# Wider idle products in round 0, later r-u-k sums and conversions, and transposes mixed with conversions in round 1: a linear-attention and MLP kernel on one core

## The chip, the core and the metric

The kernel runs on one core of a Trainium2 chip. The core has a matrix engine (TensorE, "PE" in the profile; its weight loads are listed apart as "PEld"), a vector engine (VectorE, "DVE"), a scalar engine (ScalarE, "ACT"), GpSimd ("POOL") and SyncE ("SP"), which here only issues DMAs. Each engine works through its own queue in order; they wait for each other by semaphores. The metric is the device time of one execution in microseconds, told as the median of several executions.

## What is computed

For every batch (4) and head (8), a recurrence over 768 steps with a state of 48 x 48, then a LayerNorm and a two-layer MLP with a residual:

```python
for t in range(S):
    kt, vt, rt, wt = (k[:, :, t], v[:, :, t], r[:, :, t], w[:, :, t])
    cur = np.einsum('bhd,bhe->bhde', u[None] * kt, vt)
    y[:, :, t] = np.einsum('bhd,bhde->bhe', rt, state + cur)
    state = wt[:, :, :, None] * state + np.einsum('bhd,bhe->bhde', kt, vt)
# x: y with its heads side by side, 4 x 768 x 384
xn = (x - mu) / np.sqrt(var + 1e-06) * g_ln
out = x + np.maximum(xn @ w_ch1, 0.0) @ w_ch2      # 384 -> 1536 -> 384
```

The term with `u` is the "own" term of a step: the sum over d of r, u and k, times v. All of it is in 32-bit floats.

## The kernel before

The time axis is cut into eight **rounds** (four batches, two halves of 384 steps each), and a round into two **units** of four heads. Units are numbered through: round 0 has units 0 and 1 (`u0`, `u1`), round 1 has 2 and 3, round 2 has 4 and 5.

A unit passes these stages. `turned` (line 276) transposes w, k or r of two heads on TensorE (three 128 x 128 products with the identity, names `w_ps`, `k_ps`, `r_ps`) into one of two PSUM banks and copies the result to SBUF on ScalarE (`wT`, `kT`, `rT`). `totals` (line 293) multiplies decays up into six levels (`tot`, `decay`). Then come six **levels**: `quads` (line 366) makes 24 small products of k and r into `a_ps`, `grow` (line 386) multiplies k and r by the decays of the level on VectorE, in place, and `keep` (line 401) copies the valid part of `a_ps` into the matrix `A` with a mask; at the last level these copies are put off to `finish` (ScalarE). `ends` transposes k again (`kn_ps`, `kn`), `states` makes `kv` and runs the recurrence over chunks (`s`), `exchanged` copies states to the other half of the partitions (`sx`), and `outputs` makes `y` and adds the own term (`vo`) into `x`. The own term needs the r-u-k sums: `products` (line 326) multiplies r and k on VectorE (`rk`), `product_sums` (line 340) sums them with u in 12 records of products on TensorE (`own_ps`), which ScalarE copies to `own`. For round 1 on, `moments` and `norm` prepare LayerNorm (`xn`), `turned_x` transposes it (`xT`), and `mlp` (line 562) is a generator that yields after each product group of the MLP: 12 steps for the first layer (`h_ps`, `h`), 12 for the second (`o_ps`, `o`).

The two weight matrices come into the chip in 24 parts. `fetch` (line 218) issues a part's DMA on SP into one of four `raw` buffers. `begin` (line 227) takes three ScalarE operations over a part and then fetches another; `join` (line 244) completes it with three VectorE operations. `converted` sees to it that the parts that an MLP step reads are joined first.

`warm(n)` (line 267) issues n products of zeros, 128 columns each, into a bank that nobody reads.

The order of all work is written out by hand: `InOrder` (line 39) keeps each engine's instructions in program order. Round 0 is written out in lines 648 to 721, with the transposes of round 1 (`ahead`) placed three calls at a time in levels 2 to 5. From round 1 on, a loop (line 731) goes through the levels; the rest of the work of a level is put in a list `tasks`, and `fill` (line 619) spreads it evenly between as many MLP steps as the table `UNTIL` asks for. In round 1 that list holds the `join` and `begin` calls of the level (tables `JOINS` and `BEGINS`, line 730) and then the transposes of round 2 (lines 783 to 790).

SBUF tiles come from pools by tag: `xn` has three buffers, `rk` one, `o` two. A new tile of a tag waits until the last reader of the buffer is done. `products` takes its tiles from `xn`, but the last one of unit 3 from `rk`.

Of the kernel before, what the change touches and what calls it, by code (L numbers as in the profile page):

```python
# [9 lines left out]
F32 = mybir.dt.float32  # L10
# [42 lines left out]
def kernel(  # L53
# [18 lines left out]
    B, H, S, D = r.shape  # L72
    P = 128
# [87 lines left out]
    make_identity(nc, ident)  # L161
    nought = const.tile([P, 1], F32, name="nought")
    DVE.memset(nought, 0.0)
    zeros = nought.broadcast_to([P, P])
    eps = const.tile([P, 1], F32, name="eps")
    DVE.memset(eps, 1e-6)

# [98 lines left out]

    def warm(n):

        ps = ps_m.tile([P, RN], F32, tag="m", name="idle")
        for _ in range(n):  # L270
            PE.matmul(ps[:, 0:P], zeros, zeros, start=True, stop=True)


    st, carry = {}, {}
# [51 lines left out]
    def products(q):  # L326
        a = st[q]
        a["rk"] = []
        for pr in pairs:
            if pr == NP - 1 and q == 2 * U - 1:  # L330
                rk = p1.tile([P, TT, NH, D], F32, tag="rk", name=f"rk{q}_{pr}")
                rk = rk.rearrange("p c h d -> p (c h d)")[:, 0:RN]
            else:
                rk = p3.tile([P, RN], F32, tag="xn", name=f"rk{q}_{pr}")
            DVE.tensor_tensor(
                out=rk, in0=a["r"][:, ts(pr, RN)], in1=a["k"][:, ts(pr, RN)], op=ALU.mult
            )
            a["rk"].append(rk)
# [280 lines left out]
    def fill(until, tasks):  # L619

        n = int(until) - done
        m = max(n, len(tasks))
        for i in range(m):
            for t in tasks[i * len(tasks) // m : (i + 1) * len(tasks) // m]:
                t()
            for _ in range((i + 1) * n // m - i * n // m):
                mlp_step()

    def each(f, *ranges):
        calls = [()]  # L630
        for r_ in ranges:
            calls = [c + (x,) for c in calls for x in r_]
        return [lambda c=c: f(*c) for c in calls]
# [5 lines left out]
    def units_of(rnd):  # L639
        return [U * rnd + g for g in range(U)] if rnd < NR else []  # L640
# [16 lines left out]
    grow(u0, 0)  # L657
    run(each(turned, [u1], "w", pairs))
    totals(0, DVE)
    product_sums(u0)  # L660
    for nm in "rk":
        run(each(turned, [u1], nm, pairs))
        warm(1)
    products(u1)
    quads(u1, 0)
    fetch(2)
# [1 line left out]
    run(each(load_v, [u0, u1], [SPO]) + each(load_vx, [u0, u1], [SPO]))  # L668
    begin()
    begin()  # L670
    grow(u1, 0)
    keep(0, 0)
    ahead = each(turned, new[:1], "wrk", pairs) + each(turned, new[1:], "wrk", pairs)
    for lev in range(1, NLEV):
        for q in (u0, u1):
            quads(q, lev)
        if lev == 1:
            product_sums(u1)
        else:
            run(ahead[3 * lev - 6 : 3 * lev - 3])  # L680
        if lev in (1, 3):
            begin()
        if lev == 5:
            warm(2)
        for which in ("rk",) if lev < NLEV - 1 else "kr":
            for q in (u0, u1):
                grow(q, lev, which)
        keep(0, lev)
# [7 lines left out]
    finish(2)  # L696
    states(u1)
    exchanged(u1)
    product_sums(new[0])
    load(units_of(2)[0], "w", SPO)  # L700
    own_term(u0, DVE)
    begin()
    warm(1)
    outputs(u0)
    product_sums(new[1])
    begin()
    own_term(u1, DVE)
    join()
    warm(1)
    outputs(u1)  # L710
    moments(0)
    load(units_of(2)[1], "w", SPO)
    for q in new:
# [13 lines left out]
        UNTIL.append(UNTIL[-1] + 3)  # L727
    while len(UNTIL) < NR * NLEV:
        UNTIL.append(UNTIL[-1] + MLP_STEPS // NLEV)
    JOINS, BEGINS = (3, 3, 3, 4, 4, 4), (4, 3, 1, 3, 4, 2)  # L730
    for rnd in range(1, NR + 1):
        old, now, new = units_of(rnd - 1), units_of(rnd), units_of(rnd + 1)
        if rnd == 1:
# [1 line left out]
        for lev in range(NLEV):  # L735
# [20 lines left out]
            if rnd == 1:  # L756
                if lev < 2:
                    tasks += each(load, new, "kr"[lev], [SPO])
                if lev == 2:
                    SPO.dma_start(  # L760
                        out=u_bc,
                        in_=bass.AP(
                            tensor=u.tensor, offset=u.offset, ap=[[0, P], [D, H], [1, D]]
                        ),
                    )
                    tasks += each(load_v, now, [SPO])
                if lev == 3:
                    tasks += each(load_vx, now, [SPO])
                if lev in (4, 5):
                    own_term(now[lev - 4], DVE)  # L770
                for i in range(max(JOINS[lev], BEGINS[lev])):
                    tasks += [join] * (i < JOINS[lev]) + [begin] * (i < BEGINS[lev])
            if rnd == 2 and lev == 0:
                tasks += each(load_v, now) + each(load, new, "w")
            if rnd == 2 and lev == 2:
# [5 lines left out]
            if rnd > 2 and lev < 2:  # L781
                tasks += each(load, new, ["w", "kr"][lev])
            first = 3 if rnd == 2 else 1
            if new and first <= lev < first + 3:
                due = each(turned, new, "wkr"[lev - first], pairs)
                if rnd == 1 and lev == 2:
                    due += each(turned, new[:1], "r", pairs)
                if rnd == 1 and lev == 3:
                    due = due[NP:]
                tasks += due  # L790
            if rnd == 2:
                if lev == 0:
                    tasks += each(exchanged, old)
# [17 lines left out]
            if lev == 5:  # L811
# [10 lines left out]
                if rnd >= 2:  # L822
                    tasks += each(own_sums, new[1:]) + each(own_term, new[1:], [POOL])
                    if new:
                        tasks += each(totals, [rnd + 1], [POOL])
            fill(UNTIL[slot], tasks)
            if lev == (2 if rnd == 2 else 4) and old:
                mlps.append(mlp(rnd - 1))
# [32 lines left out]
```

## Time and profile before

| | |
|---|---|
| median of 6 runs | 604.19 us (600.46 to 606.09) |
| the profiled execution | 598.02 us |
| its span, first to last instruction | 596.3 us |
| mean granted TensorE clock | 0.973 of full |
| busy: TensorE, its weight loads | 574.3 us (96%), 392.2 us (66%) |
| busy: VectorE, ScalarE, GpSimd | 295.0 us (49%), 199.6 us (33%), 70.0 us (12%) |
| first `kv` of units 0 and 1 | 46.25 and 48.47 us |
| first `h_ps` (MLP of round 0) | 62.68 us |
| first `y` of round 1 | 123.71 us |

All times inside the execution count from the start of the span. A line of the order of time reads: start, duration, engine, line of the code (here always 49, the helper that keeps the order), operation, tile written and tiles read, shape, number of records, and in brackets the idle time of the engine just before and who ended it. A product of 32-bit floats stands as two records, a transpose as one. Times of products include the latency from their issue to their end, so neighbouring groups overlap a little; distances between starts are the better measure.

### The profile page before, as it was taken

To read this page: it belongs to the slowest core of one execution; us is meant where nothing else is said; L and a number is where in the kernel's file an instruction comes from. 1 tells how busy PE (TensorE), PEld (TensorE's weight loads), DVE (VectorE), ACT (ScalarE), POOL (GpSimd) and SP (SyncE) were. 2 spreads that over 40 slices of the span, in tenths; PEclk is the share of its full clock that TensorE was granted. 3 is DMA by queue.
4 is the path that set the end of the run, shared out by engine and by line. 5 is a ranking of instruction groups with operands and counts; after the bars stand their busy time and mean duration, and the time that the engine had idled before them with its cause. 6 is when DMAs were issued, how large, how long until landed. Compare 5 with 4: busy or idle time off the path is not lost.

```text
span 596.3 us, 19140 instructions
## 1 busy us (share of the span) xinstructions
PE 574.3 (96%) x8550; PEld 392.2 (66%) x8550; DVE 295.0 (49%) x706; ACT 199.6 (33%) x430; POOL 70.0 (12%) x100
## 2 busy tenths in 40 slices
PE   8997989899999999999999999999999999999997
PEld 7887656666667766666666666667666666666554
DVE  3867988989546455445265334626245532130000
ACT  3547767702352215412343114321251015301200
POOL 5000000003170007000240007000230000000000
PEclk8759899999999999999999999999999999999999
DMA  9872788134433412232113402012000000000000
GB/s 160 185 188 69 176 215 204 41 78 88 85 58 60 91 34 41 41 72 58 33 25 62 95 14 55 2 32 58 15 2 4 15 23 6 2 14 26 0 14 26
DMA packets 122129, 36.82 MB, mean 62 GB/s; under 512 B 115776, under 2 KB 118976, under 8 KB 122048
## 3 DMA queue, kind: packets, MB, share of 16 engines
q1 hardware_dynamic: 119648, 35.31, 26.5%
q8 instruction: 67, 1.10, 0.8%
q10 hardware_dynamic: 2400, 0.30, 0.5%
q14 instruction: 14, 0.11, 0.1%
HBM read 28.51 MB, written 4.72 MB: 56 GB/s over the span
## 4 chain that ended last, share of the span: by engine, by line
PE 84%; DVE 8%; ACT 4%; issue 2%; POOL 1%; DVEq 0%; ACTq 0%; POOLq 0%
PE h_ps L49 29%; PE o_ps L49 29%; PE a_ps L49 11%; PE y L49 4%; PE r_ps L49 2%; PE k_ps L49 2%; DVE w_sb L49 2%; PE w_ps L49 2%; PE kv L49 2%; PE kn_ps L49 2%; DVE A L49 1%; PE xT_ps L49 1%; ACT rest L49 1%; DVE rT L49 1%; DVE kT L49 1%
## 5 line engine op out<-in xcount | busy, mean ns | idle before, releaser
L49 PE MATMUL o_ps<-w_sb,h 128*128 128x384 f32 x576 | 197.7, 489 | 0.1
L49 PE MATMUL h_ps<-xT,w_sb 128*128 128x384 f32 x576 | 195.8, 489 | 1.0 <-DVE w_sb L49 1.0
L49 PEld LDWEIGHTS h_ps<-xT,w_sb 128*128 128x128 f32 x576 | 105.7, 190 | 66.2 <-DVE w_sb L49 1.9
L49 PEld LDWEIGHTS o_ps<-w_sb,h 128*128 128x128 f32 x576 | 104.6, 190 | 61.7 <-issue 0.7
L49 PEld LDWEIGHTS a_ps<-rT,kT 48*64 48x64 f32 x4608 | 77.3, 140 | 20.6 <-issue 15.0
L49 PE MATMUL a_ps<-rT,kT 48*64 48x32 f32 x4608 | 82.4, 224 | 7.2 <-issue 5.2
L49 ACT ACTIVATE h<-h_ps 128x384 f32<-128x384 f32 x96 | 46.5, 489 | 122.9 <-PE h_ps L49 122.7
L49 DVE TENSOR_TENSOR o<-o_ps,x 128x384 f32<-128x384 f32 x24 | 13.4, 557 | 131.5 <-PE o_ps L49 131.4
L49 POOL TENSOR_TENSOR vo<-v,own 128x576 f32<-128x576 f32 x12 | 14.3, 1194 | 363.8 <-DVE own L49 363.8
L49 DVE COPY_PREDICATED A<-mask,a_ps 128x384 f32<-128x384 int8 x80 | 54.5, 753 | 0.0
L49 DVE TENSOR_TENSOR rT<-rT,tot 128x384 f32<-128x384 f32 x80 | 45.7, 579 | 11.2 <-PE a_ps L49 11.2
L49 DVE TENSOR_TENSOR kT<-kT,tot 128x384 f32<-128x384 f32 x80 | 45.4, 568 | 10.7 <-PE a_ps L49 10.2
L49 DVE SCALAR_TENSOR_TENSOR s<-s,decay,kv 128x48 f32<-128x48 f32 x160 | 29.3, 260 | 28.1 <-PE kv L49 28.1
L49 DVE TENSOR_TENSOR x<-y,vo 128x288 f32<-128x288 f32 x32 | 13.2, 453 | 50.1 <-PE y L49 50.1
L49 ACT ACTIVATE xT<-xT_ps,g_sb 128x384 f32<-128x384 f32 x24 | 13.7, 580 | 58.5 <-PE xT_ps L49 58.5
L49 ACT COPY rT<-r_ps 128x384 f32<-128x384 f32 x32 | 14.4, 480 | 44.0 <-PE r_ps L49 44.0
L49 ACT COPY kT<-k_ps 128x384 f32<-128x384 f32 x32 | 14.9, 479 | 38.3 <-PE k_ps L49 38.3
L49 PEld LDWEIGHTS y<-v,A 64*64 64x64 f32 x384 | 21.0, 133 | 8.2 <-issue 6.0
L49 PE MATMUL y<-v,A 64*64 64x48 f32 x384 | 23.9, 222 | 0.8 <-DVE A L49 0.8
L49 PE MATMUL y<-vx,A 64*64 64x48 f32 x384 | 23.9, 222 | 0.0
L49 ACT COPY kn<-kn_ps 128x384 f32<-128x384 f32 x32 | 14.3, 481 | 28.5 <-PE kn_ps L49 28.5
L49 PE MATMUL y<-sx,rx 48*64 48x48 f32 x384 | 23.2, 218 | 0.0
(70 smaller groups left out, 552.4 us busy)
## 6 DMA issues: line engine op xcount, KB each, us to landing
raw<-in_moe_w_ch_dram SPq DMA_DIRECT2D x24, 384.0 KB, 4.4
nat_w<-in_w_dram SPq DMA_DIRECT2D x48, 96.0 KB, 2.8
nat_k<-in_k_dram SPq DMA_DIRECT2D x48, 96.0 KB, 2.9
v<-in_v_dram SPq DMA_DIRECT2D x48, 96.0 KB, 3.2
out_dram<-o SPq DMA_DIRECT2D x24, 192.0 KB, 1.9
nat_r<-in_r_dram SPq DMA_DIRECT2D x45, 96.0 KB, 2.9
vx<-v SPq DMA_DIRECT2D x32, 72.0 KB, 2.3
nat_r<-in_r_dram ACTq DMA_DIRECT2D x3, 96.0 KB, 4.1
```

What stands on the lines that cost most here:

```text
L49: return lambda *args, **kw: self.tc.keep_in_program_order(f(*args, **kw))
```

## The change

`warm` counts in the same units of 128 columns, but issues up to three of them as one product of 384 columns. It is called at more places of round 0. The sums of unit 1 move from level 1 to behind `exchanged(u1)`, and those of units 2 and 3 each move one place back. As the `rk` tiles of unit 1 are now read later, those of units 2 and 3 go to other buffers. Two `begin` calls of round 0 move from levels 1 and 3 to levels 3 and 4. In round 1, the `begin`, `join` and `turned` calls of a level are sorted into one another by `mixed`, each kind evenly over the level, and the twelve transposing calls stand 2, 4, 4, 2 in levels 0 to 3 instead of 4, 6, 2 in levels 1 to 3; `BEGINS` has other numbers.

```diff
     def warm(n):
 
-        ps = ps_m.tile([P, RN], F32, tag="m", name="idle")
-        for _ in range(n):
-            PE.matmul(ps[:, 0:P], zeros, zeros, start=True, stop=True)
+        while n > 0:
+            m = min(n, RN // P)
+            ps = ps_m.tile([P, RN], F32, tag="m", name="idle")
+            PE.matmul(
+                ps[:, 0 : m * P], nought.broadcast_to([P, P]), nought.broadcast_to([P, m * P]),
+                start=True, stop=True,
+            )
+            n -= m
...
         for pr in pairs:
-            if pr == NP - 1 and q == 2 * U - 1:
+
+            if q == 2 and pr == 1:
                 rk = p1.tile([P, TT, NH, D], F32, tag="rk", name=f"rk{q}_{pr}")
                 rk = rk.rearrange("p c h d -> p (c h d)")[:, 0:RN]
+            elif q == 3:
+                rk = p2.tile([P, H, D], F32, tag="o", name=f"rk{q}_{pr}")
+                rk = rk.rearrange("p h d -> p (h d)")
             else:
                 rk = p3.tile([P, RN], F32, tag="xn", name=f"rk{q}_{pr}")
...
+    def mixed(*lists):
+        return [
+            t for _, t in sorted(
+                (((i + 0.5) / len(l), t) for l in lists for i, t in enumerate(l)),
+                key=lambda at: at[0],
+            )
+        ]
...
     totals(0, DVE)
+    warm(2)
     product_sums(u0)
     for nm in "rk":
         run(each(turned, [u1], nm, pairs))
-        warm(1)
+        warm(2)
...
     begin()
     begin()
+    warm(3)
     grow(u1, 0)
     keep(0, 0)
     ahead = each(turned, new[:1], "wrk", pairs) + each(turned, new[1:], "wrk", pairs)
     for lev in range(1, NLEV):
-        for q in (u0, u1):
-            quads(q, lev)
+        quads(u0, lev)
         if lev == 1:
-            product_sums(u1)
-        else:
+            warm(3)
+        quads(u1, lev)
+        if lev > 1:
             run(ahead[3 * lev - 6 : 3 * lev - 3])
-        if lev in (1, 3):
+        if lev in (3, 4):
             begin()
-        if lev == 5:
-            warm(2)
+        warm((6, 3, 2, 2, 3)[lev - 1])
...
     states(u1)
     exchanged(u1)
-    product_sums(new[0])
+    product_sums(u1)
     load(units_of(2)[0], "w", SPO)
     own_term(u0, DVE)
     begin()
-    warm(1)
     outputs(u0)
-    product_sums(new[1])
+    product_sums(new[0])
     begin()
     own_term(u1, DVE)
     join()
-    warm(1)
     outputs(u1)
+    product_sums(new[1])
     moments(0)
...
-    JOINS, BEGINS = (3, 3, 3, 4, 4, 4), (4, 3, 1, 3, 4, 2)
+    ahead = [t for nm in "wkr" for t in each(turned, units_of(2), nm, pairs)]
+    JOINS, BEGINS = (3, 3, 3, 4, 4, 4), (3, 3, 3, 3, 4, 2)
...
-                for i in range(max(JOINS[lev], BEGINS[lev])):
-                    tasks += [join] * (i < JOINS[lev]) + [begin] * (i < BEGINS[lev])
...
-            if new and first <= lev < first + 3:
-                due = each(turned, new, "wkr"[lev - first], pairs)
-                if rnd == 1 and lev == 2:
-                    due += each(turned, new[:1], "r", pairs)
-                if rnd == 1 and lev == 3:
-                    due = due[NP:]
-                tasks += due
+            if rnd > 1 and new and first <= lev < first + 3:
+                tasks += each(turned, new, "wkr"[lev - first], pairs)
...
+            if rnd == 1:
+
+                n = (1, 2, 2, 1, 0, 0)[lev] * NP
+                tasks += mixed([begin] * BEGINS[lev], [join] * JOINS[lev], ahead[:n])
+                del ahead[:n]
             fill(UNTIL[slot], tasks)
```

## The prediction

> **What bounds the kernel now.** I read the busy shares first, then the clock row, then the order of TensorE and VectorE in round 0 and round 1, and last who ended each idle stretch. From the page, two rows of forty slices of 14.9 us each:
>
> ```profile
> PE   8997989899999999999999999999999999999997
> PEclk8759899999999999999999999999999999999999
> ```
>
> TensorE is the bound nearly everywhere, and from the fifth slice on at full clock. The diff touches only rounds 0 and 1, the first 127 us; everything behind is TensorE work without slack, so what is won or lost in front reaches the end. The slices that matter are 2 to 4, where the clock is at 0.5 to 0.8. Busy time and granted clock by stretches of 3.4 us (columns: TensorE, weight loads, VectorE, ScalarE, GpSimd, clock, DMA):
>
> ```profile
> 25.20:28.60 3.40, 3.37 (x53) 2.62 (x49) 3.40 (x8) 2.47 (x6) 0.00 (x0) 0.50 0.63 118
> 28.60:32.00 3.40, 3.40 (x76) 3.01 (x72) 2.82 (x7) 0.55 (x2) 0.00 (x0) 0.50 0.80 149
> 38.80:42.20 3.40, 3.40 (x72) 3.01 (x69) 2.23 (x5) 0.71 (x2) 0.00 (x0) 0.50 0.98 344
> 42.20:45.60 3.40, 3.40 (x17) 2.93 (x16) 1.70 (x4) 1.68 (x4) 0.00 (x0) 0.50 0.72 182
> ```
>
> From 25.2 to 45.6 us TensorE is never idle and runs at half clock: 20.4 us, or six of these stretches. I chose 3.4 us because the clock changes at 8.2, 11.6, 15.0, 18.4, 25.2, 45.7, 59.3 and 62.5 us, always a multiple of about 3.4 us apart. VectorE then waits for it. The order of time of the levels (start, us, engine, operation, idle before it):
>
> ```profile
> 27.63 2.79 PE L49 MATMUL a_ps<-rT,kT 48*64 48x32 f32 x96
> 34.22 0.56 DVE L49 TENSOR_TENSOR rT<-rT,tot 128x384 f32<-128x384 f32 x1 [1.77 <-PE a_ps L49]
> 42.55 1.06 PE L49 MATMUL idle<-nought 128*128 128x128 f32 x4
> 43.41 2.69 PE L49 MATMUL kn_ps<-ident,kT 128*128 128x128 f32 x12
> 81.04 1.60 PE L49 MATMUL a_ps<-rT,kT 48*64 48x32 f32 x96
> ```
>
> The 96 quads records of a level take 2.79 us at half clock and 1.60 at full. Levels 3, 4 and 5 begin 5.02 us apart (27.63, 32.65, 37.67). In round 1 the clock is full, and the order shows two kinds of stall:
>
> ```profile
> 78.24 0.93 PE L49 MATMUL w_ps<-ident,nat_w 128*128 128x128 f32 x6 [1.77 <-ACT wT L49]
> 82.01 0.56 DVE L49 TENSOR_TENSOR rT<-rT,tot 128x384 f32<-128x384 f32 x1 [1.41 <-PE a_ps L49]
> 90.61 0.56 DVE L49 TENSOR_TENSOR rT<-rT,tot 128x384 f32<-128x384 f32 x1 [1.63 <-PE a_ps L49]
> ```
>
> The third and fourth w transposes wait for PSUM, because their copies stand behind two conversions on ScalarE (74.31 to 77.5 us). That makes the quads of level 2 late, and VectorE, gapless from 59 to 80.5, runs dry twice.
>
> **Idle products.** In units of 128 columns, `warm` now issues 2 before product_sums(u0), 1 more after each of r and k of u1, 3 before grow(u1, 0), and 3+6, 3, 2, 2, 3 in levels 1 to 5 where it had 2 in level 5; two single units behind the states go. Net: +2+2+3+19-2-2 = +22. A unit is two records: 0.43 us at half clock (42.55 to 43.41, four records), 0.21 at full by width (the 128x384 product is six records in 1.94 us, 0.65 us each). So they are 4.7 us of TensorE at full clock, 9.5 at half. Packing three units in one instruction changes no streaming time and saves some weight loads; I cost that at nothing, between 0 and -0.2 us.
>
> What they buy depends on whether they hold the clock. The idle products alone, by stretch (columns: TensorE, weight loads, clock, DMA):
>
> ```profile
> 15.00:18.40 3.40, 0.71 (x3) 0.83 (x4) 0.50 0.90 172
> 35.40:38.80 3.40, 0.00 (x0) 0.00 (x0) 0.50 0.47 79
> 42.20:45.60 3.40, 1.06 (x4) 0.98 (x4) 0.50 0.72 182
> ```
>
> Every stretch that ended with the clock going up held idle products (3.47 us of them at 1.3, 1.61 at 8.2, then 0.71, 1.06 and 1.22 at 59.3); none of the five without them did, though TensorE was busy throughout. So they do raise it. Held at full clock, level by level: quads 1.53, three transposing calls of 0.33 (six records of one kind, two calls, take 0.65), idle units 0.21 each. That is 3.2 us in level 2, 3.0 in levels 3 and 4, 3.2 in level 5. VectorE needs 4 x 0.47 for the growing and 0.95 for keeping, 2.85. TensorE remains just the bound. Level 1 stays VectorE's (22.35 to 25.93, 3.58 us) and covers its nine idle units: 1.53 + 1.92 = 3.45. If that cover fails, they cost 1.9.
>
> Before, from the quads of level 2 (23.54) to the kn transposes (43.41) is 19.9 us. After: 3.2 + 3.0 + 3.0 + 3.2 = 12.4, some 13 with the hand-overs between the two engines. Gain 6.9. The kn transposes shrink from 2.69 to 1.3, but the four ScalarE copies behind them (1.75 us in all) leave 0.8 of it. Full cover would thus give 7.7. One stretch at half clock takes back 1.7 us; I allow 0.4 of one and take **-7.0**.
>
> Here a rule speaks against the change. The Trainium skill, "TensorE: Matmul & The Clock Gate", Part 4: PE-mode transpose, says that transposes don't count as activity for the clock gate. The trace can't contradict it: at 25.2 us transposes fill 2.2 of 3.4 us and the clock stays down, and every rise had idle products in it too. If I count all streaming, levels 2 to 5 are about 70% full (level 3: 1.0 transposes + 0.43 idle + 0.64 for quads, which stream 96 x 32 columns on four tiles, in 3.0 us), far above the stretches that kept the clock (18.4 to 21.8 us with 0.34 idle and 144 quads records). By the rule, levels 3 and 4 count 1.1 us per 3.0, about what those had, and two stretches may drop. The sum is -7.0 by the first, about -4 by the second. I take the first, as idle products stand in every level.
>
> Ahead of level 1: four more units (0.85 to 1.7 us) in a part where TensorE is on the chain of waits, against a clock that may then stay up from 15.0 to 18.4 (worth up to 1.7). From -1 to +1; I take 0.
>
> **Sums of unit 1 behind kv, and of the next units later.** The 12 own_ps records (1.43 to 1.67 us of TensorE) leave level 1, where VectorE hides them: nothing gained by itself. Behind kv they take the place of those of new[0], which go behind outputs(u0), and those of new[1] go behind outputs(u1), where TensorE stands idle for 1.9 us before 59.18. The two removed idle units come off the way to outputs(u1), 0.8 us. VectorE's join ends at 55.4 while its x of unit 1 starts at 56.04, so 0.6 can be used: **-0.6**. If the own_ps behind outputs(u1) delay the xT transposes, +1 eats it. The products of units 2 and 3 go to other tiles so that unit 1's can be kept; the tiles' earlier users are done, nothing.
>
> **Conversions in round 0.** Two `begin` (1.55 us of ScalarE each) and the weight fetch that each puts on SP's queue move from levels 1 and 3 to 3 and 4. The first had waited 1.4 us for its DMA ahead of the w copies. The fetches stand behind v and vx (issued by 36.3 us), ahead of the w load of round 2. ScalarE has room: 1.4 to 3.0 busy us per level. Nothing; if copies wait for a `begin`, +0.5. DMA: the last r of unit 3 is issued by 28.4 and lands about 3 us later, needed from about 33; vx lands about 39, needed at 43.
>
> **Round 1.** `begin`, `join` and transposes are mixed; the twelve transposing calls stand 2, 4, 4, 2 instead of 0, 4, 6, 2 in levels 0 to 3. VectorE's order is unchanged. In level 0 the wT copies wait for VectorE's totals (67.4 us), and ScalarE's next `begin` and h copy behind them: some 2 us late, but joins have three begun parts in hand and the third h product's bank is free at 65.3. SP's fetches follow the begins, so loads of r come a little later; they are now needed in level 2, past 79. What goes: the 1.77 and two of 0.3 at the k and r transposes, 2.3 us of TensorE, so VectorE's 1.41 and 1.63 shrink. Behind 91 us both engines are full, so nothing more. Bounds 0 and -3.0; I take **-2.0**.
>
> **Sum:** -7.0 - 0.6 - 2.0 = -9.6. The profiled execution took 598.02 us (span 596.3), so 588.4; it lies 6.2 under the median 604.19, below all six runs (from 600.46). The same step from the median gives **594.6**.
>
> **Rivals.**
> - *A: as above*, 594.6, own range 591 to 599. Chance 0.58.
> - *B: the clock is held in part*, as the rule about transposes would have it: -4 in round 0, -0.5 and -1.5 elsewhere, 598.2. For: idle time per stretch falls to 0.43 us in levels 3 and 4. Against: the idle products stand in every level. Chance 0.22.
> - *C: next limit at once.* A load (DMA share 0.98 at 40 us) or ScalarE's copies hold kv near 44, and round 1 stays VectorE's: -3, 601.2. Against: all landing times above. Chance 0.10, half of it faster by over 0.5%.
> - *D, slower: the idle products don't hold the clock.* Then eight net units in levels 2 to 5 add 8 x 0.43 = 3.4 us to levels that TensorE bounds, and about 1.3 ahead of level 1; nothing is won elsewhere while the mixing saves little: 604.2 + 4.7 = 608.9. It decides once five of the six stretches stay at half clock. Against: the rises at 4.8, 11.6, 18.4, 45.7 and 62.5. Chance 0.10.
>
> Half a per cent (3 us) is about what can be told from no change. Faster: 0.58 + 0.19 of B + 0.05 = 0.82; same: 0.03 + 0.05 + 0.01 = 0.09; slower 0.09. The range reaches down to 587, for a round 0 that gains 8.7 with the early part and a round 1 that gains 3, and more in executions where the clock before was down for longer; and up to 602 for B and most of C.
>
> **What would show it.** The clock row at 1.0 from about 18 to the end of the kn transposes; levels 2 to 5 begin 3.0 to 3.3 us apart; kv of unit 1 near 41 instead of 48.47 us; h_ps starts near 55; no w_ps wait above 0.5 us; first y of round 1 near 114 instead of 123.7. Wrong if the row shows 0.5 through the levels, or if a gap before kv or h_ps grows.

## The result and the profile after

The changed kernel takes 599.99 us (median of 33 runs), the kernel before 602.5 us (68 runs, on the same chips). The ratio, which leaves out executions more than 1.5% above the fastest of their kernel, is 0.9952, 95% interval 0.9935 to 0.9969: 2.9 us faster, where 9.6 were forecast. Two rows of the page after, forty slices of the span each:

```profile
PE   8989997999999999999999999999999999999997
PEclk9995999999999999989999999999999999999999
```

The half-clock stretch that stood in slices 2 and 3 (the forecast's "2 to 4" misreads the row) is now in slice 4, and there is a new dip in slice 18, around 254 to 269 us, in work that the change doesn't touch. The order of time on TensorE after (start, us, engine, operation, idle before it and who ended it):

```profile
22.59 1.60 PE L49 MATMUL a_ps<-rT,kT 48*64 48x32 f32 x96
...
26.37 1.60 PE L49 MATMUL a_ps<-rT,kT 48*64 48x32 f32 x96
...
30.13 1.60 PE L49 MATMUL a_ps<-rT,kT 48*64 48x32 f32 x96
...
42.20 0.92 PE L49 MATMUL kv<-v,kn 64*64 64x48 f32 x48 [1.31 <-ACT A L49]
43.05 1.77 PE L49 MATMUL own_ps<-sel,rk 128*128 128x2 f32 x12
...
52.89 2.72 PE L49 MATMUL own_ps<-sel,rk 128*128 128x2 f32 x12
...
61.34 2.10 PE L49 MATMUL h_ps<-xT,w_sb 128*128 128x384 f32 x6
```

The quads of levels 2 to 4 take 1.60 us, the full-clock time, and begin 3.8 us apart where they began 5.0 apart. The second kv group starts at 42.20 instead of 48.47 us. But the own_ps group, 1.5 us at full clock, takes 2.72 at 52.89, and the MLP starts at 61.34, only 1.3 us earlier than before.

Marks of the executions that were traced, two of each kernel, in us from the start of the span:

| | before | before, again | after | after, again |
|---|---|---|---|---|
| second kv group | 48.47 | 47.21 | 42.20 | 42.79 |
| from there to the first h_ps | 14.2 | 17.3 | 19.1 | 18.3 |
| first h_ps to first y of round 1 | 61.0 | 63.6 | 60.0 | 62.5 |
| from there to the end | 472.6 | 472.5 | 475.9 | 476.6 |
| half clock in round 0, from 15 us on | 15.0-18.4, 25.2-45.7, 59.3-62.8 | 19.5-43.4, 50.3-60.5 | 44.1-61.2 | 45.9-63.0 |
| span | 596.3 | 600.6 | 597.3 | 600.1 |

Single executions of one kernel differ by some 5 us either way, so the verdicts below rest on the ratios of many. The spans of the two pairs differ by +1.0 and -0.5 us, and not by -2.9: the first trace of the kernel before is of one of its faster executions (598.02 us, median 602.5). So the table says where to look and not how much it is worth: some 4 to 6 us are won in the levels, 1 to 5 lost behind the states, 1 won in round 1, and 3.3 to 4.0 lost in the rest, of which the second and the last were not in the forecast.

### The profile page after: what moved, and what is told of

It reads as the page before. It is cut to its first block, busy times and chain, and to the rows that moved or that the text cites. A ratio compares the mean times of both kernels' runs of the same rounds, so it can differ in the third digit from the quotient of the medians.

```text
span 597.3 us, 19117 instructions
## 1 busy us (share of the span) xinstructions
PE 576.0 (96%) x8542; PEld 389.4 (65%) x8542; DVE 295.2 (49%) x706; ACT 198.3 (33%) x430; POOL 70.1 (12%) x100
## 4 chain that ended last, share of the span: by engine, by line
PE 85%; DVE 6%; ACT 4%; DMA 2%; issue 2%; SPq 1%; DVEq 0%
PE o_ps L49 29%; PE h_ps L49 29%; PE a_ps L49 10%; PE y L49 4%; DVE w_sb L49 2%; PE kv L49 2%; PE r_ps L49 2%; PE w_ps L49 2%; PE xT_ps L49 2%; PE k_ps L49 2%; PE idle L49 1%; PE own_ps L49 1%; PE kn_ps L49 1%; DVE A L49 1%; DVE rT L49 1%
## 5 line engine op out<-in xcount | busy, mean ns | idle before, releaser
L49 PEld LDWEIGHTS a_ps<-rT,kT 48*64 48x64 f32 x4608 | 74.7, 136 | 21.0 <-issue 13.1
L49 PE MATMUL a_ps<-rT,kT 48*64 48x32 f32 x4608 | 79.9, 221 | 5.5 <-issue 4.5
L49 DVE TENSOR_TENSOR rT<-rT,tot 128x384 f32<-128x384 f32 x80 | 45.7, 580 | 8.6 <-PE a_ps L49 8.6
L49 PEld LDWEIGHTS y<-v,A 64*64 64x64 f32 x384 | 22.9, 144 | 8.0 <-issue 6.0
L49 PE MATMUL y<-v,A 64*64 64x48 f32 x384 | 26.2, 232 | 0.8 <-DVE A L49 0.8
L49 PE MATMUL y<-vx,A 64*64 64x48 f32 x384 | 26.1, 232 | 0.0
L49 PE MATMUL y<-sx,rx 48*64 48x48 f32 x384 | 25.4, 229 | 0.0
L49 ACT COPY kn<-kn_ps 128x384 f32<-128x384 f32 x32 | 14.2, 481 | 30.3 <-PE kn_ps L49 30.3
```

Source lines behind the costliest of these rows:

```text
L49: return lambda *args, **kw: self.tc.keep_in_program_order(f(*args, **kw))
```

## The experiments

### Behind the states: which stretch decides the clock

The clock and the idle products of the changed kernel around the fall (columns as in the forecast: for the first fence TensorE, weight loads, VectorE, ScalarE, GpSimd, clock, DMA; for the second the idle products alone):

```profile
40.70:44.10 3.40, 2.09 (x73) 1.92 (x64) 3.00 (x18) 3.28 (x9) 0.00 (x0) 1.00 0.99 356
44.10:47.50 3.40, 3.40 (x93) 3.29 (x93) 1.83 (x8) 3.26 (x8) 0.00 (x0) 0.50 0.43 91
51.00:54.40 3.40, 3.40 (x75) 3.31 (x68) 1.36 (x4) 0.95 (x2) 0.00 (x0) 0.50 0.39 102
```

```profile
40.70:44.10 3.40, 0.00 (x0) 0.00 (x0) 1.00 0.99 356
44.10:47.50 3.40, 0.00 (x0) 0.00 (x0) 0.50 0.43 91
57.80:61.20 3.40, 1.22 (x2) 0.50 (x2) 0.50 0.74 184
```

In the stretch before the fall TensorE was busy for 2.09 of 3.4 us, with kv and own_ps records and no idle product; from there to 57.8 us it is busy all the time at half clock and doesn't rise until idle products come again. Four kernels ask what brings the clock down. The first puts back the two units that the change removed:

```diff
     begin()
+    warm(1)
     outputs(u0)
...
     join()
+    warm(1)
     outputs(u1)
```

> The changed kernel with one idle unit again ahead of outputs(u0) and one ahead of outputs(u1), as before the change. Theory 1 (the two removed idle units let the clock fall behind the states, from 44.1 to 61.2 us): the clock stays up, the first h_ps starts near 57.5 instead of 61.3 us, the time falls by about 3.5 us to some 596.5, ratio to before 0.990. Rival 2 (the r-u-k sums of unit 1, now behind the kv products, bring the clock down): the clock falls all the same, 600, ratio 0.995. Rival 3 (it hangs on where the gate's windows happen to lie in one execution): the median moves by less than 1 us.

Measured: 600.11 us, ratio 0.9961 (0.993 to 0.9992), as the changed kernel. In its trace the clock falls at 44.3 us all the same; the first h_ps is at 61.51. The two removed units were not it. The second fills the gap between the kv groups:

```diff
     exchanged(u0)
+    warm(6)
     finish(2)
```

> The changed kernel with six idle units between the two kv groups, where TensorE stands idle for 1.3 us waiting for the A copies; nothing else. Theory 1: the stretch that ends near 44 us then holds 1.3 us of idle products and the clock isn't lowered there; but the two stretches after it hold none, so it may fall one or two stretches later: first h_ps near 59, 598. Rival 2: no change, 600. If the gap's idle products push kv of unit 1 back they cost at most 0.2 us.

Measured: 595.99 us, ratio 0.9917 (0.9875 to 0.9959). Its clock is up to 48.5 us, down for two stretches, and the first h_ps is at 55.89. The interval still overlaps that of the changed kernel, so the time alone doesn't settle it; the traces of all the kernels of this document do, as far as the clock goes. Where the gap held no idle products behind levels that had the new ones, the clock fell between 40.2 and 46.1 us in nine traces of ten (in the tenth, of units in pieces of 128 columns, at 52.5). Where the gap was filled, it fell in none of six traces before 48.5. But it isn't the busy share of a stretch that decides. The kernel before kept its clock behind the first of these stretches (with kn_ps, 0.39 us of idle products and kv, and the same gap); the kernel with the gap filled lost it behind the second, with y and own_ps, in which TensorE was never idle:

```profile
45.69:49.10 3.41, 2.11 (x96) 1.86 (x96) 1.87 (x12) 3.29 (x8) 0.00 (x0) 1.00 0.02 5
```

```profile
45.10:48.51 3.41, 3.41 (x106) 3.34 (x105) 3.06 (x8) 3.18 (x7) 0.00 (x0) 1.00 0.23 48
48.51:51.93 3.42, 3.42 (x74) 3.40 (x75) 2.99 (x11) 1.35 (x4) 0.00 (x0) 0.50 0.84 241
```

What in the small products fails to hold the clock stays open. The third kernel moves the sums back and leaves the idle units out:

```diff
         quads(u1, lev)
+        if lev == 1:
+            product_sums(u1)
...
-    product_sums(u1)
+    product_sums(new[0])
...
-    product_sums(new[0])
+    product_sums(new[1])
...
     outputs(u1)
-    product_sums(new[1])
```

> The changed kernel with the r-u-k sums back where they were: those of unit 1 in level 1, those of units 2 and 3 ahead of outputs(u0) and outputs(u1); the idle units behind the states stay removed. Theory 1: no help, the clock falls behind the states, 600 (within 1 us). Rival 2: the clock stays up behind the states, first h_ps near 57.5, 596.5.

Measured: 600.87 us, ratio 0.9993 (0.9965 to 1.0021). The clock falls at 44.5 us as well; the second kv group is at 43.10. So the later place of the sums doesn't bring the clock down (in both kernels 12 own_ps records stand behind kv, only of different units). It may be worth up to 2.5 us (0.9993 against 0.9952, the intervals just overlap). The fourth, with the gap filled and three units (one product of 384 columns) ahead of each of the outputs:

```diff
     exchanged(u0)
+    warm(6)
...
+    warm(3)
     outputs(u0)
...
+    warm(3)
     outputs(u1)
```

> The changed kernel with six idle units in the gap between the two kv groups and three more ahead of each of outputs(u0) and outputs(u1). Theory 1b (the clock behind the states falls in the stretch with the kv gap; one idle unit elsewhere is too little, as the last runs showed): every stretch from 41 us on now holds at least 0.6 us of idle products, the clock stays up to the end of round 0, first h_ps near 55, first y of round 1 near 117, time 593 to 595, ratio 0.987. Cost of the added units if they do nothing: 6 x 0.21 on the way to outputs(u1), 1.3 us. Rival (the one with the gap alone has all that is to be had, its two half-clock stretches lie beside other waits): as that, 596 to 597.

Measured: 594.98 us, ratio 0.9887 (0.9855 to 0.992), 3.9 us better than the changed kernel and clear of it. The idle products of this kernel, and the clock (columns: TensorE, weight loads, clock, DMA):

```profile
40.70:44.10 3.40, 1.26 (x4) 0.30 (x2) 1.00 1.01 362
44.10:47.50 3.40, 0.56 (x2) 0.30 (x2) 1.00 0.44 81
47.50:51.00 3.50, 0.56 (x2) 0.00 (x0) 1.00 0.66 156
```

The clock is full to 53.0 us now, with 0.56 us of idle products in two of the stretches. That it would stay up to the end of round 0, as expected, did not come true: it is at half from 53.0 to 59.8 and again from 97.4 to 100.8 us. The first h_ps is at 55.94, where the forecast had 55, but the first y of round 1 is at 119.58 instead of the expected 117, so that of 5.4 us won at the first h_ps 1.8 are left there. Nor are the 3.9 us all the clock's: this kernel has eight product records more than the changed one, and their number matters by itself, as the section on issue waits shows. The changed kernel with the same number and an empty gap has 0.992 (0.9888 to 0.9952), which leaves some 2 us for the fillers, with intervals that overlap.

### The levels: what the idle products do there

Round 0's new idle units taken out of the changed kernel, two in level 5 as before the change, all else kept:

```diff
-        warm((6, 3, 2, 2, 3)[lev - 1])
+        if lev == 5:
+            warm(2)
```

(and the units ahead of level 1 as before the change, and those between the quads of level 1 gone.)

> The changed kernel with the new idle units of round 0 taken out (those ahead of the first sums, behind r and k of unit 1, ahead of the growing and in levels 1 to 5; two units in level 5 as before the change); the later sums, begins and the mixing stay. Theory: the clock is at half through the levels again, kv of unit 1 near 48 us instead of 42.2, and what remains is the gain of round 1 alone: about 1 us, 601.5, ratio 0.998. Rival (the later sums alone keep the clock up in the levels, as they no longer stand in level 1): kv of unit 1 near 42.

Measured: 604.51 us, ratio 1.0002 (0.9972 to 1.0032). The clock is at half from 20 to 47 us and the second kv group is at 50.72 (two issue waits of 1.44 and 2.72 us in the levels of this trace are part of that). Nothing of the change's gain is left. So the idle products are what holds the clock in the levels, not the place of the sums: it is full from 15.3 to 39.5 us in all 16 traces with the nine units of level 1, and at half for most of the levels in all four without. Next, only the ten units of levels 2 to 5 taken out:

```diff
-        warm((6, 3, 2, 2, 3)[lev - 1])
+        warm((6, 0, 0, 0, 0)[lev - 1])
```

> The changed kernel without the ten idle units of levels 2 to 5; level 1 keeps its nine. A test of whether transposes and quads by themselves keep a clock that is already up. If transposes count as activity, levels 2 to 4 are about 65% full and the clock stays up: kv of unit 1 at 42 us or earlier, time as the changed kernel or 0.5 us less. If they don't count (the rule about transposes), the clock falls within two stretches of level 2, kv of unit 1 near 46, and the time is 2 to 4 us more, or less than that if the half-clock stretches behind the states are there in both.

Measured: 602.52 us, ratio 1.002 (0.9984 to 1.0056), some 4 us slower than the changed kernel, as the second expectation had it. The levels, though, are as the first said. The clock through levels 2 to 4, and the idle products alone in the second fence (columns as above):

```profile
23.40:26.80 3.40, 3.16 (x141) 2.71 (x133) 3.40 (x8) 1.34 (x3) 0.00 (x0) 1.00 1.15 207
26.80:30.20 3.40, 3.16 (x133) 2.71 (x125) 3.40 (x9) 2.24 (x5) 0.00 (x0) 1.00 0.68 125
30.20:33.60 3.40, 3.16 (x113) 2.62 (x106) 2.97 (x7) 3.08 (x8) 0.00 (x0) 1.00 0.80 148
```

```profile
26.80:30.20 3.40, 0.00 (x0) 0.00 (x0) 1.00 0.68 125
33.60:37.00 3.40, 0.00 (x0) 0.00 (x0) 1.00 0.42 83
```

With transposes and quads alone the full clock was kept for four stretches, and the second kv group is at 39.88, 2.3 us earlier than with the ten units. The last of the four held hardly any quads. All records of it, and the quads alone (the latter view has the columns TensorE, weight loads, VectorE, ScalarE):

```profile
33.35:36.76 3.41, 2.98 (x37) 2.09 (x29) 3.27 (x8) 2.70 (x6) 0.00 (x0) 1.00 0.49 98
```

```profile
33.35:36.76 3.41, 0.33 (x19) 0.21 (x11) 0.00 (x0) 0.00 (x0) 1.00 0.49 98
```

All the rest of it is transposes, and the clock fell only one stretch later, at 40.2 us. The rule about transposes that the forecast quotes doesn't hold for keeping a clock that is up, in this execution. Raising is less regular: in the kernel before, the same work, stretched over half-clock time, didn't raise it in five stretches. But it rose behind a stretch with y and quads and no idle product in the second trace of the kernel before, at 60.5 us, and 1.22 us of idle products between 56.2 and 59.6 us didn't raise it in the second trace of the changed kernel. Where the time went all the same: as the clock fell sooner, the first h_ps is at 60.51, only 0.8 us earlier than in the changed kernel, and this kernel's end, from the first y of round 1 on, is 479.2 us long, which the next section takes up.

### The rest of the program: TensorE's issue waits

From round 2 on, all these kernels hold the same work in the same order, yet it takes from 471 to 479 us. In the order of time of the changed kernel, and below it of the kernel before, at the same work:

```profile
252.48 1.08 PE L49 MATMUL a_ps<-rT,kT 48*64 48x32 f32 x58
254.57 0.78 PE L49 MATMUL a_ps<-rT,kT 48*64 48x32 f32 x38 [1.00 <-issue]
255.28 0.55 PE L49 MATMUL k_ps<-ident,nat_k 128*128 128x128 f32 x3
255.66 3.79 PE L49 MATMUL o_ps<-w_sb,h 128*128 128x384 f32 x6
```

```profile
253.82 1.57 PE L49 MATMUL a_ps<-rT,kT 48*64 48x32 f32 x96
255.32 0.55 PE L49 MATMUL k_ps<-ident,nat_k 128*128 128x128 f32 x3
255.70 2.10 PE L49 MATMUL o_ps<-w_sb,h 128*128 128x384 f32 x6
```

After the change, TensorE stops in the middle of a quads group for 1.00 us with nothing named that it waits for ("issue"), and the six o_ps records behind it take 3.79 us instead of 2.10: the clock is at half for one stretch. Counting all product and weight-load records of TensorE ahead of each such wait of over 0.4 us gives (to within a few records):

| kernel (product records in all) | records ahead of its issue waits from round 2 on |
|---|---|
| before, both traces (8550) | 6541, 9089, 14951; in one also 12912 |
| after, both traces (8542) | 6545, 8583, 9093, 14955 |
| none in levels 2 to 5 (8534) | 6545, 8583, 9093, 11132, 14955 |
| gap and outputs (8550) | 6546, 9094, 14956 |

Between any two lie multiples of about 255 (510 = 2 x 255, 2038 = 8 x 254.8, 5862 = 23 x 254.9). The page has a DMA queue for instructions:

```profile
q8 instruction: 67, 1.10, 0.8%
```

67 packets in 1.10 MB; TensorE's 2 x 8542 records divided by 67 are 255. The times of these packets, which the traces keep, join them to the waits: each of the 82 issue waits of over 0.4 us in the 20 traces ends 1.0 to 1.7 us after a packet of this queue has landed. (In the changed kernel one starts at 252.18 us and lands at 253.11; the wait above ends at 254.57.) So, as far as these counts and times show, TensorE gets its instructions in blocks of that size, and where a block's edge falls into a run of small products, it runs out of them. But then each product added or saved in round 0 moves all edges behind it. Packing three units in one product, and adding units, the change alters the count by 16 instructions, and one more edge (8583) falls into quads. Two kernels test it. The changed kernel with four narrow products more, so that it has the count of the kernel before:

```diff
     warm(8)
+    ps = ps_m.tile([P, RN], F32, tag="m", name="idle")
+    for _ in range(4):
+        PE.matmul(
+            ps[:, 0:32], nought.broadcast_to([P, P]), nought.broadcast_to([P, 32]),
+            start=True, stop=True,
+        )
```

> The changed kernel with four more products of zeros, 32 columns wide, right behind the first warm(8), where TensorE waits for the first loads of w anyway: 8550 product records, as many as the kernel before, where the changed kernel has 8542. All traces with 8542 to 8546 records show an issue wait near 254 us and a half-clock stretch behind it, none with 8550. Theory (TensorE's instructions come in blocks, about 255 records and weight loads counted together lie between two issue waits, and the change moved the blocks' edges into other groups of small products): no issue wait near 254, first y of round 1 to the end 472.5 to 473.5 us instead of 476, time 597, ratio 0.990. Rival (the count is a coincidence): 600, ratio 0.995, the wait near 254 is still there.

And the kernel before with four products fewer, of the same width in sum:

```diff
-    warm(8)
+    ps = ps_m.tile([P, RN], F32, tag="m", name="idle")
+    for n in (3, 3, 1, 1):
+        PE.matmul(ps[:, 0 : n * P], zeros, nought.broadcast_to([P, n * P]), start=True, stop=True)
```

> The kernel before with its first eight idle units issued as products of 384, 384, 128 and 128 columns instead of eight of 128: same streaming, four products fewer, 8542 records. Theory: an issue wait near 254 us appears with a half-clock stretch behind it, in work that the edit doesn't touch; first y of round 1 to the end 475.5 to 476.5 us instead of 472.5, time 3 us more, ratio 1.005. Rival (the count is a coincidence): ratio 1.000 and no such wait.

Measured: the first 598.16 us, ratio 0.992 (0.9888 to 0.9952) against the changed kernel's 0.9952; the second 606.04 us, ratio 1.0046 (1.0012 to 1.008), slower than the kernel it came from. The order of time of the second, in work that its edit doesn't touch:

```profile
253.84 0.98 PE L49 MATMUL a_ps<-rT,kT 48*64 48x32 f32 x56
256.20 0.79 PE L49 MATMUL a_ps<-rT,kT 48*64 48x32 f32 x40 [1.38 <-issue]
```

and of the first:

```profile
257.38 1.57 PE L49 MATMUL a_ps<-rT,kT 48*64 48x32 f32 x96
258.88 0.55 PE L49 MATMUL k_ps<-ident,nat_k 128*128 128x128 f32 x3
259.26 2.10 PE L49 MATMUL o_ps<-w_sb,h 128*128 128x384 f32 x6
```

The wait comes with the count and goes with it. From the first y of round 1 to the end the second took 475.8 us (before: 472.6), as expected, the first 474.3 (after: 475.9 and 476.6), where 472.5 to 473.5 was expected; its trace had a half-clock stretch at 196 us, behind another wait. The slowdown of the second is clear of noise; the gain of the first is not, as its interval overlaps that of the changed kernel.

All 20 traces fit one sum. The time from the first y of round 1 to the end, less the issue waits in it, less half of the time that it spends at half clock, is 467.9 to 469.8 us. And each of the 19 falls of the clock in that part, but for the program's last microseconds, comes within 1.5 us of the end of an issue wait; which of the waits has one behind it changes from trace to trace. In the kernel with the sums back, the wait near 254 us is there and no fall.

The width of the idle products acts on the count too. The changed kernel with the same units in pieces of 128 columns:

```diff
-            m = min(n, RN // P)
+            m = 1
```

> The changed kernel with the same number of idle units at the same places, issued as products of 128 columns again. Theory: streaming time is the same, so the clock and the time are the same within 1 us, ratio 0.995. Rival (the clock gate counts columns streamed and not weight loads, so narrow products hold it less well): the clock falls within the levels, some 2 us or more slower.

Measured: 602.69 us, ratio 1.0001 (0.9972 to 1.0031), slower than the changed kernel, if barely clear of it, although the clock was up through the levels in its trace and the first h_ps at 55.58. It has 8594 product records and issue waits after 7055, 10877, 12917, 13427 and 15465. A second trace:

> The changed kernel with idle units in pieces of 128 columns once more. The first trace had the first h_ps at 55.6 us, better than the changed kernel's, and 479.1 us from the first y of round 1 to the end with 5.5 us of issue waits, worse than any but one. If the long tail belongs to this kernel's instruction stream, again about 479, which would explain its slower median; if it hangs on the execution, anywhere from 471 to 479.

It had the same five counts; the first h_ps was at 61.53, with the clock at half from 46.1 to 63.2 us, where the first trace has one stretch from 52.5 on. So how long the clock is down behind the states hangs partly on the execution. The end took 476.3 us (479.0 in the first, with one half-clock stretch more). A fifth wait may explain part of the slower median; two traces don't show that it explains all. Second traces of the other two, in the table at the start:

> The changed kernel once more, for a second trace. If the half-clock stretch behind the states belongs to the kernel, the clock is at half from about 44 to 61 us again and the first h_ps starts near 61.3; if it hangs on the execution, it starts anywhere from 55 to 62. From the first y of round 1 to the end it took 475.9 us with 4.5 us of issue waits: if those belong to the kernel, again 475 to 477.

> The kernel before once more: first trace 62.7 us to the first h_ps, half clock from 25.2 to 45.6, 472.6 us from the first y of round 1 to the end with 3.2 us of issue waits. If kernel-bound: the same within 1 us. If it hangs on the execution: other stretches at half clock and another tail.

The places of the issue waits belong to the kernel. The half-clock stretches hang partly on the execution: the second trace of the kernel before has three behind the states, from 50.3 to 60.5 us, which the first did not have. So the length of the end hangs on both. The two traces of each kernel happen to agree (472.6 and 472.5; 475.9 and 476.6), but the seven traces with 8550 product records, of all kernels, range from 472.5 to 476.3 (mean 474.4) and the six with 8542 from 474.4 to 476.6 (mean 475.7).

### Round 1

A wait of 3.15 us at o_ps is new in round 1. First ScalarE, then TensorE, of the changed kernel:

```profile
96.44 0.53 ACT L49 ACTIVATE w_sb<-raw 128x384 f32<-128x384 f32 x1
98.61 1.22 ACT L49 ACTIVATE rest<-raw 128x384 int32<-128x384 uint32 x2 [1.63 <-DVE w_sb L49]
99.70 0.46 ACT L49 ACTIVATE h<-h_ps 128x384 f32<-128x384 f32 x1
```

```profile
100.21 3.49 PE L49 MATMUL o_ps<-w_sb,h 128*128 128x384 f32 x10 [3.15 <-ACT h L49]
```

A `begin` waits for a `join` on VectorE to free a rest tile, and the h copy, which o_ps needs, stands behind it on ScalarE. The old counts of begins:

```diff
-    JOINS, BEGINS = (3, 3, 3, 4, 4, 4), (3, 3, 3, 3, 4, 2)
+    JOINS, BEGINS = (3, 3, 3, 4, 4, 4), (4, 3, 1, 3, 4, 2)
```

> The changed kernel with the old counts of begins in round 1 (4, 3, 1, 3, 4, 2), the mixing kept. In the changed kernel ScalarE waits 2.7 and 1.6 us for a join before it can write the next rest tile, and an h copy stands behind it: TensorE waits 3.15 us at o_ps. Theory: the three begins of level 2 make every later begin wait for the newest join; with one begin there the waits go, o_ps waits under 0.5 us, and the time falls by 2 to 3 us to some 597.5. Rival (VectorE is full there anyway, the wait hides it): under 0.5 us.

Measured: 598.65 us, ratio 0.9966 (0.9944 to 0.9987). The o_ps wait is gone and the time is not better: in this trace TensorE waits 1.18 us for VectorE at kn_ps, which it didn't before, so that VectorE's work seems to set the pace there. The same edit in the kernel with gap and outputs filled:

> The same with the old counts of begins in round 1 as well. If the o_ps wait of 3.15 us costs anything, this is 1 to 2 us faster than the one without it, 592 to 593; if VectorE bounds that part anyway, within 0.7 us of it.

Measured: 593.6 us, ratio 0.9882 (0.9818 to 0.9947), no difference from 0.9887. With joins sorted ahead of begins there, and counts 3, 3, 2, 3, 4, 3:

> The kernel with idle units in the gap and ahead of the outputs, mixed round 1, but joins sorted ahead of begins at the same place and one begin moved from level 2 to level 5 (3, 3, 2, 3, 4, 3). If ScalarE's wait for a join comes from begins running up to the limit of four rest tiles, the o_ps wait falls from 3.1 to under 1 us, first h_ps to first y is about 59 us, and the time is 593. If VectorE bounds that part, within 0.7 us of 595.

Measured: 594.39 us, ratio 0.9883 (0.9839 to 0.9926), again none. Then round 1 wholly as before the change, first in the kernel with gap and outputs filled (both have 8550 product records), then in the changed kernel (both 8542):

```diff
+                for i in range(max(JOINS[lev], BEGINS[lev])):
+                    tasks += [join] * (i < JOINS[lev]) + [begin] * (i < BEGINS[lev])
...
-                tasks += mixed([begin] * BEGINS[lev], [join] * JOINS[lev], ahead[:n])
```

(with the old counts and the old levels of the transposes.)

> The kernel with idle units in the gap and ahead of the outputs, with round 1 wholly as before the change (old order of joins, begins and transposes, old counts): what the mixing is worth by itself. Forecast's theory: round 1 as mixed is 2 us shorter, so this is 2 us slower than with mixing, 597. Rival (the 3.1 us wait at o_ps that the mixed order brings, and the half-clock stretch that follows it in several traces, give the gain back): within 1 us, 594 to 596; first h_ps to first y of round 1 about 61 us, as before the change.

> The changed kernel with round 1 wholly as before the change (order of joins, begins and transposes, and their counts); round 0 as changed. If the forecast's -2.0 for round 1 holds, this is 2 us slower than the changed kernel, 602, ratio 0.9985. If the mixing costs what the last comparison suggests (591.7 without it against 595.0 with it), this is 2 to 3 us faster than the changed kernel, 597.5, ratio 0.991. If it is worth nothing either way: 600, 0.995.

Measured: 591.73 us, ratio 0.9845 (0.9797 to 0.9893, six runs), against 0.9887 with the mixing; and 600.48 us, ratio 0.999 (0.9966 to 1.0014), against 0.9952 with it. The signs are opposite: in the changed kernel the mixing is worth some 2.3 us, with the clock held behind the states it costs some 2.5, and in both pairs the intervals overlap. What it is worth by itself stays open. The first of the two, 9 to 10 us under the kernel before, is the fastest version found, on six runs. With its idle units in pieces of 128 columns:

> The fastest version so far (idle units in the gap and ahead of the outputs, round 1 as before the change), its idle units issued in pieces of 128 columns. The changed kernel lost some 3 us by such pieces, though its one trace showed the clock up through the levels. If the width matters for the clock: 594 to 595, ratio 0.989. If that loss was of the kernel's spread: within 1 us of 591.7, ratio 0.984.

Measured: 594.98 us, ratio 0.9894 (0.9834 to 0.9954, six runs), not clear of the other. Its trace has only two issue waits from round 2 on, and the shortest end of all, 470.8 us.

## Why the prediction was right or wrong

**The idle products hold the clock in the levels: right.** -7.0 for the time to the kv products; they came 6.3 us earlier in the first pair of traces, 4.4 in the second. Quads took 1.60 us, as forecast. Levels lay 3.8 us apart instead of 3.0 to 3.2. In the first of them the transposes take 1.5 us with a wait of 0.24 for a copy, where I put 1.0, and the three idle units 0.74, where I put 0.63; the time that I gave a level was too small by that. The ten units of levels 2 to 5 weren't needed in the one trace without them. And "they do raise it" was read from one trace: in others the clock rose without idle products, or didn't rise with them.

**"The two removed idle units come off the way to outputs(u1) ... -0.6": wrong, and the larger part of the miss in round 0.** The step that failed is the full clock behind the states, which this term takes for granted. From the second kv group to the first h_ps the changed kernel took 19.1 and 18.3 us, the kernel before 14.2 and 17.3. I had asked of every level whether its stretches would keep the clock, and did not ask it of the part behind the states, where kv, sums and y are small products and the kv gap stays 1.3 us. Filling the gap brought the first h_ps from 61.3 to 55.9 us. With fillers ahead of the outputs, and the old count of records besides, the ratio was 0.9887, 6.8 us of the forecast 9.6; that its median, 595.0 us, is near my 594.6 is luck, as I had started from a median of 604.19 that is 602.5 over more runs. The removed units by themselves were not the cause, as putting them back showed.

**"Packing three units in one instruction ... I cost that at nothing", and "what is won or lost in front reaches the end": wrong.** The count of instructions moved the edges of TensorE's instruction blocks in rounds 2 to 7, and an issue wait, mostly with a half-clock stretch behind it, came up near 254 us: 2.8 us when the kernel before was given the same count (ratio 1.0046, 1.0012 to 1.008), 1.9 when the changed kernel was given the old one (0.992 against 0.9952, the intervals overlap). The 3.3 and 4.0 us of the two pairs of traces also hold what half-clock stretches chance to add. The sign had stood in the profile before. Where I wrote that TensorE "stands idle for 1.9 us before 59.18" and counted it as room, the line reads:

```profile
59.18 0.35 PE L49 MATMUL a_ps<-rT,kT 48*64 48x32 f32 x9 [1.92 <-issue]
```

It was an issue wait in the middle of a quads group. Nor does what is won in front all reach even the first y of round 1: with the gap and the outputs filled, 1.8 of 5.4 us did, with the clock at half up to 59.8 and from 97.4 to 100.8 us.

**Round 1, -2.0: the waits went as forecast, the size is not shown.** The w_ps wait of 1.77 us is gone, and so are VectorE's two of 1.41 and 1.63, though a new one of 1.95 us follows at 104.6. First h_ps to first y fell by 1.0 and 1.1 us in the traces, and undoing round 1 alone cost 2.3 us, with intervals that just overlap. The wait at o_ps, which I had not seen coming, cost nothing that the runs show. That the worth seems to turn with the state of round 0 (+2.3 and -2.5 us, neither clear of noise) speaks against adding parts up, but doesn't prove it.

**The rivals.** B's total (-6.0) and C's (-3) were nearer, and C's number is that of the result, by luck: of its mechanism the levels show only waits of 0.2 to 0.4 us for copies and one of 0.25 for a load. B's outcome, a clock held in part, is what happened, but not by its mechanism: the clock fell behind the levels, and transposes kept it in the one trace that tested it.

## What to carry to other kernels

The clock changed here only at multiples of about 3.4 us, and it has to be held in each such stretch, not only where the profile shows half clock now: when work moves forward, ask of each later stretch what fills it, even where TensorE looks busy, and put fillers into waits that are there anyway. Adding or saving instructions on an engine can cost microseconds far behind the edit; before a small change is judged, compare the issue waits, and the time of the untouched rest, in both traces. And a part may be worth 2 us in one version and cost 2 in the next, so the parts of a reordering are best tried again in the version that is to stay. One trace of each version is too little for differences of this size, as the half-clock stretches move from execution to execution.

## What was unexpected of the hardware

- TensorE's issue waits lie about 255 records or multiples of it apart and come at the same counts in both traces of a kernel (but for one of 0.49 us). The 77 of over 0.4 us behind the first y of round 1, in 20 traces, took 0.5 to 1.9 us each, and each ends 1.0 to 1.7 us after a packet of the instruction queue has landed. In the changed kernel, one left the clock at half for the next 3.4 us, so that six o_ps records took 3.79 us instead of 2.10.
- Whether a full clock is kept is not a matter of TensorE's busy time: it was kept behind a stretch busy for 2.11 of 3.41 us and lost behind one busy throughout with y and own_ps. Transposes with 0.33 us of quads kept it.
- In one trace a half clock was not raised by five stretches of unbroken work with transposes and quads; in another the same work kept a full clock for four stretches.
